# Eight weight copies instead of six behind the last token product: moving two weight loads of a fused recurrence and soft-MoE kernel

## The chip, the cores and the metric

The kernel runs on one core of one Trainium2 chip. The metric is the device time of one execution in microseconds (us). Four executions of the kernel before took 200.65, 200.97, 200.97 and 200.61 us, median 200.81 us. The core has five engines that run their own instruction streams: TensorE (PE in the profile; PEld is its weight load), VectorE (DVE), ScalarE (ACT), GpSimd (POOL) and SyncE (SP), which here only issues transfers. Transfers run on 16 DMA engines; in the profile q1 carries what SP issues, q0 what POOL issues.

## The reference

Two stages follow each other. The first is a gated recurrence over 5056 tokens for each of 4 sequences and 256 channels; the second is a soft mixture of experts over all 20224 tokens with 8 experts of 4 slots each.

```
f = lower_bound + (1 - lower_bound) * sigmoid(f_logit)
for t in range(S):  h = f[:, t] * h + (1 - f[:, t]) * x[:, t];  y[:, t] = h

logits = y @ phi                              # 20224 x 32
d = exp(logits);  d /= d.sum(over tokens)
slot_input = d.T @ y                          # 32 x 256
per expert e: slot_out = relu(slot_input[e] @ w1[e]) @ w2[e]
c = exp(logits);  c /= c.sum(over slots)
out = c @ slot_out
```

No output row can be written before the last token has gone through the recurrence, into `slot_input`, and through all experts. The expert weights `w1` (8 x 256 x 1024) and `w2` (8 x 1024 x 256) are 1 MB each per expert in float32, and are needed only then.

## The kernel before

**Units.** Tokens go in groups of 512 (`G`) per sequence; one group of one sequence is a *unit*, numbered n = 4 * group + sequence, so there are 40 units (0 to 39). A loop over n runs the stages of several units at once, shifted against each other. In the steady state iteration n issues, in this order: the loads of units n+6 and n+7 (`load`, lines 177 to 193, even n only, on SP); the sigmoid of units n+4 and n+5 on ACT (`gate`, line 203); the product of the sigmoid and x for unit n+3 on POOL (`enter`, line 214); weight copies, if any, on POOL (`load_w`, lines 128 to 134); then on PE the transposes of h of unit n-1 back to tokens (`to_tokens`, line 275), of the sigmoids of n+2 and n+3 and the product of n+1 to channels (lines 223 to 229); the decay factors on ACT (line 252); the recurrence itself as two scans of unit n on DVE (`scan`, line 262), 1.24 us each; the copy of unit n-1's tokens out of PSUM (line 292, DVE or ACT); and by groups the logits, exponentials and slot sums (lines 306, 315, 327 to 330, 356). Each engine executes its stream in the order in which the program writes it.

**Token buffers.** f and x arrive in tiles of two units; each of the two tags has three tiles (`ld`, line 149). The last x load, of units 38 and 39, is issued at n = 32 and takes the tile that the products of units 32 and 33 release; that release comes at n = 30.

**Weights.** There are 16 weight matrices, `w1[0..7]` and then `w2[0..7]`. `load_w(i)` issues a copy with a cast from float32 to bfloat16, from POOL, into a tile of its own; the last matrix is copied in two halves, so there are 17 copies. How many are issued at which iteration stands in the table `W_AT` (line 143), and a counter takes them in order:

```
            unit(enter, n + 3)
            for _ in range(W_AT.get(n, 0)):
                load_w(w_next[0])
                w_next[0] += 1
```

So the copies of iteration n stand behind the product of unit n+3 in POOL's stream. In the table of before, iterations 17 and 25 take `w1[0]` and `w1[1]`, 30 to 34 take `w1[2]` to `w2[1]`, and 36, behind the product of unit 39 (the last one), takes `w2[2]` to `w2[7]`. At most eight POOL transfers can be in flight: the program uses eight semaphores in turn for them, and a copy waits for the landing of the one eight before it.

**After the units.** Behind those copies POOL clears two tiles (`hid` and `wide`, lines 517 and 518) and copies the last 64 tokens' weights (`left`, line 349). PE finishes the last group's logits and slot sums, bridges waits with small matmuls whose result nobody uses (`spin`, line 139), then multiplies by the experts: line 566 with all of `w1`, line 602 with `w2[0..3]`, line 612 with `w2[4..7]` in four blocks of eight matmuls (j = 0 to 3, one matrix each; the last block waits for the halves of `w2[7]` separately). Between blocks j = 1 and j = 2 PE computes the row sums (line 339) and 14 spin matmuls. Line 627 (DVE) makes `slot_out`, on which all of the output depends. The output stage (lines 643 to 738) then multiplies `slot_out` into all tokens and writes 20.7 MB.

Of the kernel before, what the change touches and what calls it, by code (L numbers as in the profile page):

```python
# [18 lines left out]
def kernel(  # L19
# [108 lines left out]
    def load_w(i):  # L128
        if i < E:
            nc.gpsimd.dma_start(out=w1_sb[i], in_=w1_r[i])  # L130
        else:
            k = FC // 2 if i == 2 * E - 1 else FC
            for f in range(0, FC, k):
                nc.gpsimd.dma_start(out=w2_sb[i - E][:, ds(f, k)], in_=w2_r[i - E][:, ds(f, k)])
# [5 lines left out]
                             start=True, stop=True, skip_group_check=True)  # L140

    SPINS = 14
    W_AT = {17: 1, 25: 1, 30: 1, 31: 1, 32: 1, 33: 2, 34: 3, 36: 6}
    w_next = [0]
    ctx.enter_context(tc.manual_schedule())

# [3 lines left out]
    with tc.tile_pool(name="sp2", bufs=3) as sp2, \  # L150
# [211 lines left out]
        def unit(f, m):  # L362
            if 0 <= m < n_unit:
                f(m)
# [63 lines left out]
        for n in range(n_unit):  # L428
# [14 lines left out]
            else:  # L443
# [16 lines left out]
# [3 lines that stand above are left out]
# [306 lines left out]
```

## Time and profile before

| | |
|---|---|
| median of 4 executions | 200.81 us (200.61 to 200.97) |
| the profiled execution | 200.65 us, of it 198.9 us span |
| PE, DVE, ACT, POOL busy | 143.3, 142.4, 137.8, 102.5 us |
| read, written in HBM | 58.23 MB, 20.71 MB |
| q1 (token loads, outputs) | 62.13 MB, 76.6% of 16 engines' span |
| q0 (weights) | 8.42 MB counted at the destination, 21.1% |
| mean granted TensorE clock | 0.854 |

All positions below are microseconds from the start of the span. A line of a timeline reads: start, length, engine, line of the code, instruction, count, and in brackets how long the engine sat idle before it and what released it. A line of a table by stretches reads: stretch, its length, busy time and count of PE, PEld, DVE, ACT and POOL, the granted PE clock, the busy share of the DMA engines (values a little over 1.00 are to be read as full), and GB/s counted at the destination. For the casting weight copies the destination is half the source. A line of waits reads: who waited, for whom, total us, times, longest.

### The profile page before, as it was taken

Reading aid. Unit: us, or ns where it says so; the run is one execution under the profiler, and the core shown is the slowest. Engines: PE = TensorE matmul, PEld = TensorE weight load, DVE = VectorE, ACT = ScalarE, POOL = GpSimd, SP = SyncE. Lnnn points to the kernel's source line nnn. Section 1 sums busy time; section 2 is a strip of 40 time slices with the busy share of each in tenths; the row PEclk is TensorE's granted clock in tenths of the full one; section 3 lists DMA queues with packets and bytes.
Section 4 is the critical chain, followed back from the end, with each engine's and each line's share of the span. In section 5 each row is a group of like instructions: output and inputs, shape, how many; then the busy total and the mean of one; then the engine's idle time right before and its main releaser. Section 6 shows DMA issues by size and latency. Waiting matters only on the chain.

```text
span 198.9 us, 3264 instructions
## 1 busy us (share of the span) xinstructions
PE 143.3 (72%) x1201; PEld 103.6 (52%) x1201; DVE 142.4 (72%) x164; ACT 137.8 (69%) x194; POOL 102.5 (52%) x77
## 2 busy tenths in 40 slices
PE   0587594987978889778978565989989999950000
PEld 0365473965766769566866454666953643310000
DVE  2669878699999999999999978415168878840000
ACT  3688665999999999899985791434059889980000
POOL 2489596874999399947998547860030000000000
PEclk9999969699999999999999999799996555555555
DMA  5999999999999999999999999999629999999995
GB/s 187 415 419 420 422 417 419 420 419 417 416 420 419 335 392 419 416 361 356 413 369 273 283 247 216 214 213 212 127 96 425 421 436 422 428 458 428 422 422 214
DMA packets 17759, 70.76 MB, mean 356 GB/s; under 512 B 2112, under 2 KB 3136, under 8 KB 16848
## 3 DMA queue, kind: packets, MB, share of 16 engines
q1 hardware_dynamic: 15120, 62.13, 76.6%
q0 software_dynamic: 2480, 8.42, 21.1%
q8 instruction: 9, 0.15, 0.3%
q14 instruction: 6, 0.05, 0.1%
q10 hardware_dynamic: 144, 0.00, 0.0%
HBM read 58.23 MB, written 20.71 MB: 397 GB/s over the span
## 4 chain that ended last, share of the span: by engine, by line
PE 27%; DMA 25%; DVE 23%; issue 5%; ACT 3%; POOL 3%; SPq 1%; ACTq 0%; DVEq 0%; POOLq 0%
DVE h L262 19%; DMA x_t<-in_x_dram 15%; PE op L696 11%; DMA f_t<-in_f_logit_dram 11%; DVE ht L292 3%; POOL u_t L214 3%; PE op L647 2%; PE hp L275 2%; PE so_ps L612 2%; PE tail L139 1%; ACT oc L707 1%; ACT ob L641 1%; SPq L193 1%; PE up L229 1%; PE tail L339 1%
## 5 line engine op out<-in xcount | busy, mean ns | idle before, releaser
L214 POOL TENSOR_TENSOR u_t<-s_t,x_t 128x1024 bf16<-128x1024 bf16 (+1 forms) x39 | 82.4, 2129 | 26.0 <-ACT s_t L203 12.5
L262 DVE TENSOR_TENSOR_SCAN h<-a,h,up 128x512 bf16<-128x512 f32 (+1 forms) x72 | 85.8, 1244 | 3.8 <-PE up L229 2.3
L203 ACT ACTIVATE s_t<-f_t 128x2048 bf16<-128x2048 f32 (+2 forms) x23 | 38.6, 1677 | 10.4 <-DMA f_t<-in_f_logit_dram 10.4
L252 ACT ACTIVATE a<-sp,nomlb 128x1024 f32<-128x1024 bf16 (+2 forms) x46 | 43.3, 993 | 3.4 <-PE sp L229 3.0
L275 PE MATMUL hp<-ident_f,h 128*128 128x128 f32 (+1 forms) x160 | 30.6, 317 | 16.3 <-DVE ht L292 12.6
L275 PEld LDWEIGHTS hp<-ident_f,h 128*128 128x128 f32 (+1 forms) x160 | 23.3, 209 | 25.8 <-DVE ht L292 16.6
L229 PE MATMUL sp<-ident_f,s_t 128*128 128x128 f32 x144 | 21.0, 288 | 12.0 <-ACT s_t L203 9.0
L229 PE MATMUL up<-ident_f,u_t 128*128 128x128 f32 x144 | 24.0, 292 | 2.6 <-POOL u_t L214 2.5
L696 PE MATMUL op<-slot_bd,etall 64*128 64x512 bf16 x62 | 24.0, 586 | 0.6 <-ACT oc L707 0.3
L229 PEld LDWEIGHTS sp<-ident_f,s_t 128*128 128x128 f32 x144 | 16.9, 148 | 14.0 <-issue 5.8
L707 ACT ACTIVATE oc<-op,rrow 128x256 f32<-128x256 f32 x60 | 22.7, 488 | 1.5 <-PE op L696 0.9
L701 DVE TENSOR_TENSOR oc<-op,rrow 128x1024 f32<-128x1024 f32 x16 | 19.2, 1220 | 4.7 <-PE op L696 4.6
L229 PEld LDWEIGHTS up<-ident_f,u_t 128*128 128x128 f32 x144 | 18.2, 151 | 4.1 <-POOL u_t L214 3.6
L292 DVE COPY ht<-hp 128x512 f32<-128x512 f32 (+1 forms) x22 | 14.6, 666 | 4.1 <-PE hp L275 3.9
L696 PEld LDWEIGHTS <-etall 64*128 64x128 bf16 x62 | 9.0, 153 | 14.2 <-issue 11.7
L168 PE MATMUL slot_ps<-rep,ident 128*128 128x256 bf16 x112 | 16.2, 279 | 0.0
L292 ACT COPY ht<-hp 128x512 f32<-128x512 f32 (+1 forms) x18 | 10.6, 586 | 6.9 <-PE hp L275 6.8
L168 PEld LDWEIGHTS <-ident 128*128 128x128 bf16 x118 | 11.7, 103 | 1.9 <-issue 0.6
L641 ACT ACTIVATE ob<-op,rrow 128x256 f32<-128x256 f32 x16 | 6.3, 479 | 8.9 <-PE op L647 8.8
L262 DVE TENSOR_TENSOR_SCAN h<-a,up 128x512 bf16<-128x512 f32 x8 | 9.4, 1210 | 2.7 <-ACT a L252 2.0
L629 POOL TENSOR_SCALAR slot_bd<-slot_out,parity 128x256 bf16<-128x256 bf16 x2 | 1.8, 920 | 13.2 <-DVE slot_out L627 13.2
L306 PE MATMUL lg<-h,phi 128*32 128x512 bf16 (+1 forms) x80 | 7.7, 433 | 0.0
(99 smaller groups left out, 128.4 us busy)
## 6 DMA issues: line engine op xcount, KB each, us to landing
f_t<-in_f_logit_dram SPq DMA_DIRECT2D x36, 512.0 KB, 9.9
x_t<-in_x_dram SPq DMA_DIRECT2D x36, 512.0 KB, 9.9
out_dram<-oc SPq DMA_DIRECT2D x6, 2048.0 KB, 13.2
w_sb<-in_moe_w_dram POOLq DMA_DIRECT2D x15, 512.0 KB, 12.2
out_dram<-oc SPq DMA_DIRECT2D x4, 896.0 KB, 5.9
out_dram<-ob SPq DMA_DIRECT2D x1, 2048.0 KB, 8.9
f_t<-in_f_logit_dram SPq DMA_DIRECT2D x4, 384.0 KB, 9.1
x_t<-in_x_dram SPq DMA_DIRECT2D x4, 384.0 KB, 7.9
```

The costliest lines, as they stand in the source:

```text
L168: nc.tensor.matmul(slot_bank[:, 1, ds(0, rhs.shape[1])], ident, rhs, start=first and i < 2, stop=False, skip_group_check=True)
L203: nc.scalar.activation(s_t, f_t, ACT.Sigmoid, scale=-1.0)
L214: nc.gpsimd.tensor_tensor(uts[n][:, :r], s_t[:, :r], x_t[:, :r], ALU.mult)
L229: nc.tensor.transpose(ps[:, :, r], t[:, r], ident_f)
L252: nc.scalar.activation(decays[n // 2, o][:, ds(n % 2, k), :T], sp[:, ds(n % 2, k), :T, o], ACT.Identity, scale=nomlb[:, ds(o, 1)], bias=1.0)
L262: nc.vector.tensor_tensor_scan(h[:, :T, o], decays[n // 2, o][:, n % 2, :T], up[:, :T, o], hs[n - B][:, ds(used(n // B - 1) - 1, 1), o] if ...
L275: nc.tensor.transpose(hp[:n_p, r], hw[:, :n_p, r], ident_f)
L292: copy(hts[g][:n_p, b].rearrange("p r d -> p (r d)").bitcast(F32), hps.pop(n)[:n_p].rearrange("p r c -> p (r c)"))
L641: nc.scalar.activation(ob[:, i], op[:, i], ACT.Copy, scale=scale[:, i])
L696: nc.tensor.matmul(op[:, i_r].rearrange("p u d -> p (u d)"), ew[:, :, r + i_r], slot_bd[ds(j * 2 * NS, 2 * NS)].rearrange("s u d -> s (u d)"),
L701: nc.vector.tensor_tensor(ob[:, :, ds(r, k)].rearrange("p u r d -> p r u d"), op[:, ds(0, k)], scale[:, ds(r, k)].unsqueeze(3).broadcast_t ...
L707: nc.scalar.activation(ob[:, u, r + i_r], op[:, i_r, u], ACT.Copy, scale=scale[:, r + i_r, ds(u, 1)])
```

## The change

The table loses its entries for iterations 30 and 31, and the entry for 36 grows from 6 to 8.

```diff
-    W_AT = {17: 1, 25: 1, 30: 1, 31: 1, 32: 1, 33: 2, 34: 3, 36: 6}
+    W_AT = {17: 1, 25: 1, 32: 1, 33: 2, 34: 3, 36: 8}
```

Since the counter takes the matrices in order, the copies themselves keep their order, and the last `w2[7]` stays last. What changes is the place of each in POOL's stream: iterations 32 to 34 now take `w1[2]` to `w1[7]` (before: `w1[4]` to `w2[1]`), and all eight `w2` matrices, nine copies, stand behind the product of unit 39. The products of units 34 to 37 have two copies fewer before them. The instruction streams of PE, DVE, ACT and SP are the same, instruction for instruction.

## The prediction

> **What bounds the kernel now.** I read the chain of work that ended last first, in order of time (start, length, what).
>
> ```profile
> 99.21 21.05 DMA x_t<-in_x_dram
> 120.27 0.02 issue
> ...
> 120.42 2.16 POOL u_t L214
> ...
> 143.17 1.76 PE so_ps L612 x16
> 144.93 0.03 issue
> 144.96 0.06 DVE slot_out L627
> ```
>
> The last x load is on the chain for 21.05 us, against a median of 9.9 us for such loads; POOL's last product, PE's tail and `slot_out` at 144.96 follow. From there to the end everything hangs on `slot_out`. So the question is how much earlier `slot_out` comes. POOL's timeline shows what the load shared the DMA engines with:
>
> ```profile
> 98.75 0.57 POOL L130 DMA_DIRECT2D w_sb<-in_moe_w_dram  x1
> ...
> 101.44 0.58 POOL L130 DMA_DIRECT2D w_sb<-in_moe_w_dram  x1
> ...
> 110.84 1.07 POOL L134 DMA_DIRECT2D w_sb<-in_moe_w_dram  x2
> 116.69 2.14 POOL L214 TENSOR_TENSOR u_t<-s_t,x_t 128x1024 bf16<-128x1024 bf16 x1 [4.78 <-DMA x_t<-in_x_dram]
> 120.42 2.15 POOL L214 TENSOR_TENSOR u_t<-s_t,x_t 128x1024 bf16<-128x1024 bf16 x1 [1.59 <-DMA x_t<-in_x_dram]
> 122.51 3.23 POOL L134 DMA_DIRECT2D w_sb<-in_moe_w_dram  x6
> 126.41 0.53 POOL L134 DMA_DIRECT2D w_sb<-in_moe_w_dram  x1 [0.67 <-DMA w_sb<-in_moe_w_dram]
> ```
>
> Eight copies go out between 98.75 and 111.9. The products of units 38 and 39 wait 4.78 and 1.59 us for x. The last copy waits 0.67 us for an earlier one. The third view is the DMA by stretches:
>
> ```profile
> 100.00:120.00 20.00, 14.16 (x118) 11.51 (x115) 18.00 (x18) 15.24 (x16) 13.31 (x12) 1.00 1.06 288
> ...
> 126.00:128.00 2.00, 2.00 (x19) 1.30 (x18) 0.69 (x1) 0.73 (x2) 1.59 (x3) 0.74 1.08 217
> ...
> 142.00:144.00 2.00, 2.00 (x32) 1.90 (x31) 0.76 (x2) 0.00 (x0) 0.00 (x0) 1.00 0.27 49
> 144.00:146.00 2.00, 1.79 (x15) 1.28 (x13) 0.48 (x1) 0.00 (x0) 0.39 (x1) 1.00 0.03 8
> ```
>
> The reader is to see the second bound: the DMA engines are full from before 100 until about 142.5, and go idle only when the last weight is in. When that lands is read from SP, whose first output waits for the weights' memory:
>
> ```profile
> SPq L673 <- DMA w_sb<-in_moe_w_dram: 43.6, 2, 41.2
> ```
>
> SP issued its last load until 99.64 (98.84 plus 0.80). 41.2 us later, at 140.85, one matrix is in; the second wait adds 2.4, so the last half lands at 143.25. By the semaphores' order these are `w2[6]` and `w2[7]`. PE needs that last half for the last four of the 16 matmuls that end at 144.93, at 110 ns each, so from 144.49. The slack between weight stream and compute chain is 144.49 - 143.25 = 1.24 us. Two bounds lie that close together, and the change helps only one.
>
> **The change part by part.**
>
> *DMA work, conserved.* Nothing is removed. A weight (524 KB at the destination) takes 524/213 = 2.46 us alone (213 GB/s in the stretches from 120 on, DMA full), a load 524/420 = 1.25 us (about 420 GB/s in the load-only slices). After 120 the stretches move 4.73 MB, 9.0 weights; 14 went out from 98.75 on, so 5.0 passed between 100 and 120 (2.61 MB), and 5.75 - 2.61 = 3.14 MB were loads. Alone these would take 12.26 + 7.48 = 19.74 of the 20 us: mixing costs at most 0.26. Serving loads first therefore moves the end of the stream by 0 to 0.26 us earlier, if the engines never run dry. I take 0: landing stays at 143.25.
>
> *Does the stream run dry?* Without the copies at 98.75 and 101.44, the 3.14 MB of loads last until at least 107.5, and the copy of iteration 32 goes out near 102.8. The next five go out by 111.9 as before, since the product of unit 36 already waits 0.71 us for PE at 104.94 and absorbs what POOL gains. Six weights are 14.8 us of work; with the loads they fill the engines until 100 + 7.5 + 14.8 = 122.3. The nine `w2` copies can start when the product of unit 39 ends, about 116.3 (below). Margin 6 us.
>
> *Token loads.* Before x of unit 39 there are two weights fewer, 4.9 us: it lands at 115.4 instead of 120.27, and nearer 114 if the sharing stays as between 104 and 112 (272 to 289 GB/s, so weights about 70% of the time). The product of unit 38 can follow the copies at 112.0, that of 39 at 114.1 to 115.4, ending at 116.3 to 117.5 instead of 122.57.
>
> *What is late next.* DVE, by its timeline:
>
> ```profile
> 116.36 2.45 DVE L262 TENSOR_TENSOR_SCAN h<-a,h,up 128x512 bf16<-128x512 f32 x2 [1.30 <-PE up L229]
> 118.73 0.66 DVE L292 COPY ht<-hp 128x512 f32<-128x512 f32 x1
> 120.03 0.69 DVE L330 COPY et<-ep 128x1024 bf16<-128x1024 bf16 x1 [0.63 <-PE ep L327]
> 120.64 2.44 DVE L262 TENSOR_TENSOR_SCAN h<-a,h,up 128x512 bf16<-128x512 f32 x2
> ```
>
> Its 1.30 us wait goes back, through PE's transposes, to the sigmoid of units 38 and 39:
>
> ```profile
> ACT s_t L203 <- DMA f_t<-in_f_logit_dram: 1.2, 1, 1.2
> ```
>
> f of unit 39 is ahead of both x loads, so this wait goes; the exponentials and the token copy behind the sigmoid on ACT come 1.2 us earlier too. The 0.63 before line 330 goes with POOL's lateness, since PE's transposes of line 327 stood behind the late product of unit 38. With the 0.24 us before the scan of unit 39, DVE's last scan ends 1.3 to 2.1 us earlier (I take 1.9). PE's last long wait, 1.23 us for the product of unit 39 at 122.63, is replaced by DVE's line 330, ending 119.0; PE resumes its tail at 119.65 instead of 122.63, 2.98 us earlier. From there to `hi_ps` PE was busy nearly throughout, so 1.3 to 3.0 of it reach the experts. I take 2.9, as the scan then ends well before the logits of unit 39 need it.
>
> *Weights at the experts.* Counting back 2.46 us per matrix from 140.85, `w2[5]` lands at 138.4, `w2[4]` at 135.9, `w2[3]` at 133.5. Line 602 moves from 137.69 to 134.8 and finds its four; block j = 0 ends near 136.8; j = 1 waits for 138.4 and ends at 139.3; row sums (1.3) and spin (0.8) end at 141.4; j = 2 has `w2[6]` and ends at 142.3; the first half of j = 3 ends at 142.75, and the second waits for 143.25. It ends at 143.25 + 0.06 + 0.44 = 143.75 instead of 144.93. **Of 2.9 us, 1.18 remain.** Were the compute gain only 1.3, the result would be the same.
>
> *POOL.* Two issues of 0.57 leave the stretch to 102; two of 0.54 join behind unit 39. There the memsets, `left` and `slot_bd` queue behind them. The last copy waits, before and after, for the landing of `w2[0]` near 126 (eighth before it), which covers the 1.08 us, and the memsets still end near 131.4. If that cover is gone they end at 132.5; `wide` is first written at 137.84 - 2.9 = 134.9. The cost is 0 either way. SP's and ACT's queues are not passed.
>
> *Two rules against rows.* The weights run at 213 GB/s. The Trainium skill, "DMA: Bandwidth & Descriptors", section "Anatomy of one DMA — SWDGE (gpsimd) path", gives about 2 us plus bytes over 436 GB/s, an estimate of 1.2 us of engine time per copy; by it the stream would end long before line 612 and the whole 2.9 us would show, 197.7 us. The measured rate decides. The other rule is in the clock rival.
>
> **Sum.** Output stage and all after it shift by 1.18: 200.65 - 1.18 = 199.47 us for an execution like the profiled one. That execution lay 0.16 under the median of 200.81; the same shift from the median gives 199.63. I say 199.6.
>
> **The rivals.**
>
> *1. The clock (slower).* PE now waits about 1.6 us for `w2[5]`. The row: PE was busy 2.73 of the 6.1 us from 116.5 to 122.6, its longest gap 1.23 us, and the clock fell to 0.50 at about 123.6 for 3.6 us. If it falls at 138.4, j = 1, row sums, spin and j = 2, 3 (4.8 us) take up to 9.6: PE ends near 147.9, 3.0 later, 203.6 us. It decides if the clock falls before about 141; falling later, the gain merely shrinks. Against: from 136 to 141 PE would still be busy about two thirds, and a stretch with 0.71 busy of 3.2 us (111.6 to 114.8) kept the clock at 1.00. The Trainium skill, "TensorE: Matmul & The Clock Gate", section "HAM oscillation — how this bites in real kernels", asks for no idle gap over about 3.4 us; the trace fell with shorter ones. By that rule 1.6 us cost nothing. Middle price +1.5: 202.1.
>
> *2. The stream ends later (no change).* If the product of unit 39 ended after 122.3, the engines would idle, and each microsecond delays `w2[7]` and the end by one. A landing 0.8 to 1.5 us later gives 200.3 to 201.1. For: all nine copies now hang on that product. Against: the 6 us margin.
>
> *3. It does little for the tokens.* The six copies of 32 to 34 still run beside the last loads and take most of the time; if x of unit 39 lands after 119, the chain gains under 1 us: 199.9 to 200.6. Against: f and x of four units were ahead of any weight.
>
> *4. More than the forecast.* If mixing and the uneven last 1.5 us of the stream shrink, the landing comes 0.3 to 0.7 earlier: 198.9 to 199.3.
>
> **How the numbers follow.** Forecast 0.62 (199.2 to 200.1); clock 0.10; later stream 0.14; little for the tokens 0.06; more 0.08. About 0.2% (0.4 us) is what a measurement can tell from no change. Faster takes the forecast, rival 4, half of rival 3 and a little of rival 2: 0.75. Same: the rest of 3 and most of 2: 0.13. Slower: the clock and the end of 2: 0.12. The range runs from 199.0 to 201.0: out stay the clock's and the lowest values.
>
> **What would show it.** POOL's waits for x at units 38 and 39 mostly gone; DVE's 1.30 us gone; PE's last `hi_ps` block 2 to 3 us earlier; in line 612 a new wait for a weight; SP's wait for the weights ending again near 143.2; `slot_out` near 143.8. Wrong if the weights land later than 144, or the clock is under 1.00 between 137 and 144.

## The result and the profile after

The changed kernel takes 200.2 us in the median of 53 executions, the kernel before 200.97 us in the median of 79. The medians are 0.77 us apart. The ratio of the two is 0.9971, 95% interval 0.9959 to 0.9983: 0.3% faster, or 0.34 to 0.82 us. An execution over 1.5% above the fastest of its kernel is left out of a ratio, here and below (five of the ten of `no4_before`, at most two elsewhere). The forecast was 199.6 us, a gain of 1.18 us. The direction and the mechanism came out as forecast; about half of the gain did not come.

The profiled execution took 200.05 us, its span is 198.3 us. Its chain of work that ended last (start, length, what) no longer has a token load near the end:

```profile
113.40 4.18 POOL u_t L214 x2
117.58 8.81 DMA w_sb<-in_moe_w_dram
126.39 0.28 issue
126.67 16.97 DMA w_sb<-in_moe_w_dram
143.68 0.61 PE so_ps L612 x4
```

Where the last x load stood for 21.05 us, the chain now has two weight copies, and the last four matmuls of line 612 start when the second lands. POOL's timeline (start, length, instruction, idle before) shows why:

```profile
113.38 4.26 POOL L214 TENSOR_TENSOR u_t<-s_t,x_t 128x1024 bf16<-128x1024 bf16 x2 [1.69 <-PE hp L275]
117.58 3.23 POOL L134 DMA_DIRECT2D w_sb<-in_moe_w_dram  x6
121.72 0.53 POOL L134 DMA_DIRECT2D w_sb<-in_moe_w_dram  x1 [0.91 <-DMA w_sb<-in_moe_w_dram]
...
126.67 0.53 POOL L134 DMA_DIRECT2D w_sb<-in_moe_w_dram  x1 [1.91 <-DMA w_sb<-in_moe_w_dram]
```

The products of units 38 and 39 run back to back from 113.38 with no wait for x (before: 4.78 and 1.59 us); what holds them now is a wait of 1.69 us for PE. The nine copies behind them go out from 117.58. The last three each wait for a landing, and the last one goes out at 126.67, 0.26 after its place in the trace of before. DVE has no gaps left up to the last scan:

```profile
112.40 4.92 DVE L262 TENSOR_TENSOR_SCAN h<-a,h,up 128x512 bf16<-128x512 f32 x4
117.23 0.67 DVE L292 COPY ht<-hp 128x512 f32<-128x512 f32 x1
117.86 0.69 DVE L330 COPY et<-ep 128x1024 bf16<-128x1024 bf16 x1
118.47 4.78 DVE L262 TENSOR_TENSOR_SCAN h<-a,h,up 128x512 bf16<-128x512 f32 x4
```

The 1.30, 0.63 and 0.24 us waits are gone, and the last scan ends at 123.25 instead of 125.77. On PE the waits for weights took their place:

```profile
136.35 1.03 PE L612 MATMUL so_ps<-w_sb,wide 128*128 128x256 bf16 x8 [2.13 <-DMA w_sb<-in_moe_w_dram]
...
138.68 1.03 PE L612 MATMUL so_ps<-w_sb,wide 128*128 128x256 bf16 x8 [0.86 <-DMA w_sb<-in_moe_w_dram]
...
141.68 1.47 PE L612 MATMUL so_ps<-w_sb,wide 128*128 128x256 bf16 x12
143.68 0.60 PE L612 MATMUL so_ps<-w_sb,wide 128*128 128x256 bf16 x4 [0.53 <-DMA w_sb<-in_moe_w_dram]
```

Before, line 612 had no such wait. The expert stage starts far earlier (`hi_ps` at 129.55 instead of 134.11, 4.56 us), and most of that is given back in these three waits, 3.52 us together; another 0.40 is lost around them. `slot_out` starts at 144.32 instead of 144.96: 0.64 us, which is also the difference of the two spans (198.9 and 198.3). The DMA engines are full as before and go idle at the same place (stretch, length, busy times, PE clock, DMA share, GB/s):

```profile
100.00:120.00 20.00, 15.12 (x139) 12.44 (x138) 19.89 (x21) 14.86 (x16) 16.72 (x17) 1.00 1.06 290
...
142.00:144.00 2.00, 1.47 (x14) 1.17 (x12) 0.64 (x2) 0.00 (x0) 0.00 (x0) 1.00 0.17 32
```

They moved 290 GB/s between 100 and 120 against 288, and 32 against 49 in the last stretch: the end of the stream has hardly moved.

### The profile page after: what moved, and what is told of

It reads as the page before. It is cut to its first block, busy times and chain, and to the rows that moved or that the text cites. A ratio compares the mean times of both kernels' runs of the same rounds, so it can differ in the third digit from the quotient of the medians.

```text
span 198.3 us, 3264 instructions
## 1 busy us (share of the span) xinstructions
PE 142.9 (72%) x1201; PEld 103.7 (52%) x1201; DVE 142.3 (72%) x164; ACT 137.7 (69%) x194; POOL 102.5 (52%) x77
## 4 chain that ended last, share of the span: by engine, by line
DMA 31%; DVE 23%; PE 18%; ACT 8%; issue 7%; POOL 2%; ACTq 0%; DVEq 0%; SPq 0%; POOLq 0%
DVE h L262 18%; DMA w_sb<-in_moe_w_dram 13%; PE op L696 12%; DMA f_t<-in_f_logit_dram 10%; DMA x_t<-in_x_dram 8%; ACT a L252 3%; DVE ht L292 3%; POOL u_t L214 2%; PE op L647 2%; ACT s_t L203 2%; PE hp L275 1%; DVE ob L637 1%; ACT ht L292 1%; PE sp L229 1%; ACT L203 1%
## 5 line engine op out<-in xcount | busy, mean ns | idle before, releaser
L275 PE MATMUL hp<-ident_f,h 128*128 128x128 f32 (+1 forms) x160 | 29.6, 309 | 16.5 <-DVE ht L292 12.0
L275 PEld LDWEIGHTS hp<-ident_f,h 128*128 128x128 f32 (+1 forms) x160 | 22.8, 208 | 25.8 <-DVE ht L292 15.8
L229 PE MATMUL sp<-ident_f,s_t 128*128 128x128 f32 x144 | 22.3, 300 | 9.8 <-ACT s_t L203 7.5
L229 PEld LDWEIGHTS sp<-ident_f,s_t 128*128 128x128 f32 x144 | 18.0, 154 | 11.7 <-issue 5.7
L292 DVE COPY ht<-hp 128x512 f32<-128x512 f32 (+1 forms) x22 | 14.7, 670 | 1.7 <-PE hp L275 1.7
L168 PE MATMUL slot_ps<-rep,ident 128*128 128x256 bf16 x112 | 15.7, 273 | 0.0
```

The source lines that it names most:

```text
L168: nc.tensor.matmul(slot_bank[:, 1, ds(0, rhs.shape[1])], ident, rhs, start=first and i < 2, stop=False, skip_group_check=True)
L229: nc.tensor.transpose(ps[:, :, r], t[:, r], ident_f)
L275: nc.tensor.transpose(hp[:n_p, r], hw[:, :n_p, r], ident_f)
L292: copy(hts[g][:n_p, b].rearrange("p r d -> p (r d)").bitcast(F32), hps.pop(n)[:n_p].rearrange("p r c -> p (r c)"))
```

## Experiments

**Is the changed kernel bounded by the last weight, and the kernel before by the tokens?** The copies of `w2[4..7]` are taken away from both kernels, and line 612 multiplies by `w2[3]` in their place: the four matrices are left out of the output, the number of matmuls stays.

```diff
-    W_AT = {... 36: 8}          # before: 36: 6
+    W_AT = {... 36: 4}          # before: 36: 2
...
-                                 w2_sb[Q + j][:, fc],
+                                 w2_sb[Q - 1][:, fc],
```

> The changed table without the copies of w2[4..7]; the matmuls of line 612 use w2[3] instead, so the instruction count on TensorE stays and the last four experts' part of the output is computed from the wrong matrix. Theory (the changed kernel waits for the last weight, its compute chain is 3 to 4 us ahead): line 612 no longer waits, slot_out comes near 140.2 instead of 144.32 (34 matmuls, row sums and spin straight behind line 602 at 134.2), about 4.1 us less: 196.1 us. Rival (the compute chain is what ends last in the changed kernel too): at most 0.3 us less than the changed kernel.

> The table of before without the copies of w2[4..7], line 612 on w2[3]. Theory (before, the tokens bound, the weights land 0.9 to 1.2 us before they are needed): slot_out stays at 144.9, time within 0.3 us of the kernel before, since all eight copies ahead of the last tokens are still there. Rival (the weight stream bounded the kernel before as well): 3 to 4 us less.

The changed kernel without them: 196.43 us, ratio to before 0.9782 (0.9726 to 0.9838), 4.4 us. PE's timeline shows line 612 directly behind line 602, and DVE's shows `slot_out`:

```profile
134.28 1.05 PE L612 MATMUL so_ps<-w_sb,wide 128*128 128x256 bf16 x8
...
138.60 1.91 PE L612 MATMUL so_ps<-w_sb,wide 128*128 128x256 bf16 x16
```

```profile
140.55 0.48 DVE L627 TENSOR_SCALAR slot_out<-so_ps,rcs 128x256 bf16<-128x256 f32 x1 [0.99 <-PE so_ps L612]
```

So the changed kernel's compute chain is 3.8 us ahead of its weights, as the theory had it (4.1). The kernel before without the four copies: a median of 200.55 us over ten executions between 197.85 and 202.52, 0.36 under the 200.91 of the kernel before beside it; ratio 0.9927 (0.9877 to 0.9976). That is far from the 3 to 4 us of the rival, but past the "within 0.3" of the theory, a little by the medians and clearly by the ratio. In its profile `slot_out` starts at 143.60, 1.36 before the 144.96 that I had taken for the kernel before, with x still late (4.29 us wait). Of this, 0.26 us is an earlier start: PE begins the transposes of unit 39 (line 229) at 122.37 instead of 122.63. The other 1.10 lie between there and `hi_ps`, 10.39 us instead of 11.49. The rows by stretches show why; the first is of the kernel before, the others of this run:

```profile
123.50:127.20 3.70, 3.70 (x39) 2.15 (x40) 2.28 (x2) 1.80 (x4) 3.03 (x7) 0.54 1.06 213
```

```profile
114.00:116.00 2.00, 1.46 (x7) 1.46 (x8) 1.32 (x2) 1.97 (x3) 0.00 (x0) 0.62 1.09 272
116.00:118.00 2.00, 2.00 (x12) 1.75 (x11) 0.60 (x1) 2.00 (x4) 1.54 (x1) 0.53 1.08 246
123.50:127.20 3.70, 3.70 (x53) 2.46 (x53) 2.93 (x3) 2.42 (x6) 3.70 (x2) 1.00 1.06 214
```

The granted clock fell around 114.5 to 118 here, where TensorE waits for x anyway, and stayed at 1.00 from 123.5 to 127.2, where it was 0.54 in the trace of before: 53 matmuls passed there instead of 39. The stretch from line 229 of unit 39 to `hi_ps` takes 10.39 to 10.42 us in all eleven profiles of this document without a fall in it, 11.49 in that of before and 11.94 in that of `one_back` (below), which have one. So the end of the compute chain of the kernel before moves by more than a microsecond between executions. Where it ends early, that kernel too would meet the weights, and the change has less to win.

**How far does one have to go, and what is too far?** Only the table is changed, in both directions.

```diff
-    W_AT = {17: 1, 25: 1, 32: 1, 33: 2, 34: 3, 36: 8}
+    W_AT = {17: 1, 25: 1, 29: 1, 30: 1, 31: 1, 32: 1, 33: 2, 34: 3, 36: 5}   # one_ahead
+    W_AT = {17: 1, 25: 1, 31: 1, 32: 1, 33: 2, 34: 3, 36: 7}                 # one_back
+    W_AT = {17: 1, 25: 1, 32: 1, 33: 2, 36: 11}                              # three_more
```

> The opposite direction: one more copy ahead of the last tokens (one at 29, five at 36). Theory (on this side of the optimum the tokens end last, and each copy ahead of them is worth its 2.46 us of transfer time): x of unit 39 lands near 122.7 instead of 120.3, slot_out at 146.5 to 147.4, 1.5 to 2.5 us slower than before. Rival (only the end of the weight stream matters, since total transfer work is fixed): no change from before.

> Only the entry at 30 is moved: 31 keeps one copy, 36 takes seven. Theory (gain capped by the landing of the last weight, which one moved copy already reaches): tokens about 2.2 us earlier than before, last weight lands at 143.5 to 143.7, slot_out near 144.3 as in the full change, time 0.5 to 0.7 us below before. Rival (each moved copy brings its share): half the gain, 0.3 us.

> The three copies of 34 go behind the last product too: 36 takes eleven. Theory (total transfer work is fixed, so the stream ends later only by the time the DMA engines run dry): loads and the three remaining copies are worth 14.9 us from 100, the eleven are issued from about 117.3, so the engines are dry for 3 to 4.5 us, the last weight lands at 147 to 148, time 2.5 to 4 us above before. Rival (the tokens still bound, moving more copies helps more): equal to the changed kernel or faster.

| copies behind unit 39's product | median us | ratio to before | `slot_out` in the profile |
|---|---|---|---|
| 5 (one_ahead) | 203.88 | 1.0132 (1.0067 to 1.0197) | 148.63 |
| 6 (before) | 200.97 | 1 | 144.96 |
| 7 (one_back) | 200.39 | 0.9974 (0.9944 to 1.0004) | 144.54 |
| 8 (the change) | 200.2 | 0.9971 (0.9959 to 0.9983) | 144.32 |
| 11 (three_more) | 206.07 | 1.0253 (1.0177 to 1.0329) | 151.15 |

The ratios are to executions of the kernel before in the same run, with medians of 200.67 (5 copies) and 200.91 us (7 and 11). With 7 copies the last four matmuls wait for the same landing, by PE's timeline:

```profile
143.90 0.60 PE L612 MATMUL so_ps<-w_sb,wide 128*128 128x256 bf16 x4 [0.53 <-DMA w_sb<-in_moe_w_dram]
```

So the first moved copy already reaches the floor and the second adds nothing that can be measured, as the theory said (the interval of this run alone, though, would also admit the rival's half gain, or none; the trace decides). With 5 copies POOL waits longer for x than before:

```profile
121.45 2.14 POOL L214 TENSOR_TENSOR u_t<-s_t,x_t 128x1024 bf16<-128x1024 bf16 x1 [7.63 <-DMA x_t<-in_x_dram]
```

The product of unit 39 follows at 125.17. x came 4.75 us later, nearly twice the 2.46 that I had priced for one copy, and the time went past the 1.5 to 2.5 expected. The DMA queues show that the price was the wrong one. Between 100 and 104 the loads moved 0.77 MB here against 1.27 MB before. Beside copies they moved 1.62 MB in the 12 us from 104 to 116 of the trace of before, 0.135 MB per us, and at that rate the missing 0.50 MB take an estimated 3.7 us to catch up, not the 1.2 that they need alone. The release of the x tile is 0.6 later too (the loads go out at 99.44). How much of the rest is chance stays open: in the profile of `fill_before` (below), the same program as before up to that point, the products of units 38 and 39 also start 1.65 us later than in the trace of before.

With 11 copies the stream runs dry:

```profile
114.00:116.00 2.00, 1.38 (x13) 1.06 (x11) 1.98 (x2) 1.99 (x4) 2.00 (x2) 1.00 0.47 92
116.00:118.00 2.00, 1.63 (x16) 1.48 (x16) 2.00 (x4) 2.00 (x3) 2.00 (x2) 1.00 0.00 0
118.00:120.00 2.00, 1.27 (x22) 1.06 (x23) 2.00 (x4) 0.28 (x1) 2.00 (x5) 1.00 0.47 41
```

The DMA engines stand idle for about 4.1 us (1.06 + 2.00 + 1.06 of these six), which is the forecast size of that term. The last half then lands at 148.8 (issued at 131.31, 17.5 us by the list of transfers), past the 147 to 148 expected and 5.3 later than before. `slot_out` is 6.19 later in this profile (206.79 us, the slowest of four executions). The clock adds to the landing: from 136.6 to 150.3 it was at 0.50, PE waited for one matrix after another, and the last 16 matmuls of line 612 took 2.94 instead of 1.91 us, to 151.11.

**What has slack?** 18 more idle matmuls (1.95 us at full clock) stand where the changed kernel waits, and at the same place in the kernel before.

```diff
         for j in range(Q):
+            if j < 2:
+                spin(tail[:, 1], (12, 6)[j], D)
             for fc in range(FC):
                 nc.tensor.matmul(so_ps, wide[:, fc, j]...
```

> The changed kernel with 18 more idle matmuls of 256 columns on TensorE (1.95 us at full clock): 12 ahead of block j = 0 and 6 ahead of j = 1 of line 612, where it waits for weights. Theory (TensorE has 3 to 4 us to spare before the last weight): slot_out stays at 144.3, the added work costs nothing; and if the upper group of executions (200.9 to 201.7, 12 of 53) comes from the clock falling while TensorE waits for weights, that group thins out and the median falls by up to 0.3 us. Rival (TensorE's chain bounds the changed kernel): 1.5 to 2 us slower.

> The same 18 idle matmuls in the kernel before. Theory (before, the compute chain ends last): the 1.95 us lie on the path, slot_out at 146.5 to 146.9 instead of 144.96, 1.5 to 2 us slower than before. Rival (the weights bound the kernel before too): no change.

In the changed kernel they cost nothing: 199.96 us, ratio 0.9949 (0.9924 to 0.9974), `slot_out` at 144.11. In the kernel before they cost 1.0% (ratio 1.01, 1.0062 to 1.0137), 2.0 us, with `slot_out` at 147.47. That is 2.51 after the 144.96 of before and past the 146.5 to 146.9 expected: beside the 1.95 of the added work, line 602 already starts 0.55 later, since x came 1.65 later and the clock did not fall between line 229 and `hi_ps`. The same work is free in one and fully paid in the other, which shows the two bounds more directly than any wait. Executions of `fill` lay between 199.66 and 200.89, while the changed kernel on the same chip had two of twelve above 201; that fits the clock as a cause, but twelve executions don't show it.

**Can the last wait be shortened?** The last matrix comes in pieces of 4, 3 and 1 blocks, so that less work hangs on the last landing; then both edits together.

```diff
-            k = FC // 2 if i == 2 * E - 1 else FC
-            for f in range(0, FC, k):
+            f = 0
+            for k in (FC // 2, FC // 2 - 1, 1) if i == 2 * E - 1 else (FC,):
                 nc.gpsimd.dma_start(out=w2_sb[i - E][:, ds(f, k)], ...)
+                f += k
```

> The changed kernel with w2[7] copied in three pieces (4, 3 and 1 of its eight blocks) instead of two halves. Theory (after the last landing only the matmuls that need it are left): one matmul follows the landing instead of four, 0.3 us less than the changed kernel, slot_out near 144.0. Rival (the third copy's own fixed cost, or its 1 KB runs, delays the landing by as much): equal or up to 0.3 us slower.

> The changed kernel with both edits: w2[7] in pieces of 4, 3 and 1 blocks, and 18 idle matmuls where line 612 waits. Theory: slot_out near 143.8 as with the pieces alone, 0.4 to 0.7 us below the changed kernel; the idle matmuls take away executions above 200.9. Rival (the pieces' gain was spread between executions): equal to the changed kernel.

> The changed kernel once more, as the reference for the next three on the same chip. Both theories: 0.2 to 0.4% faster than before. In its profile the last half of w2[7] lands at 143.4 to 143.9 and the last four matmuls of line 612 follow it at once.

> The changed kernel a third time, as the reference on the same chip: 0.2 to 0.4% faster than before; the last half of w2[7] lands between 143.4 and 143.9.

The pieces alone: 199.67 us beside 200.3 of the changed kernel on the same chip; ratios to before 0.9945 (0.9912 to 0.9977) and 0.9971 (0.9942 to 1.0001). Both edits: 199.65 us beside 200.4, ratios 0.9928 (0.9897 to 0.9958) and 0.9983 (0.9944 to 1.0023). All twelve executions of `fill_split` lie between 199.27 and 199.81; the changed kernel's beside it between 199.75 and 202.64. PE's timeline of `fill_split` (line numbers moved by three):

```profile
143.19 0.62 PE L615 MATMUL so_ps<-w_sb,wide 128*128 128x256 bf16 x4 [0.18 <-DMA w_sb<-in_moe_w_dram]
```

The four matmuls start when the piece of three blocks is in; the last piece lands at 143.48 (issued at 128.78, 14.7 us by the list of transfers), and only the fourth needs it. `slot_out` starts at 143.85, 0.47 before the changed kernel's 144.32. From the last landing to `slot_out` 0.37 us pass instead of 0.68, which is the 0.3 us expected for fewer matmuls behind it; the other 0.16 is an earlier last landing, within what the profiles differ by. This version beats both kernels: eleven of the changed kernel's twelve executions took longer than its slowest, and so did all 23 of the kernel before in that run.

In the third profile of the changed kernel the rival of the clock came true, by the stretches:

```profile
136.00:138.00 2.00, 1.53 (x8) 1.10 (x9) 0.00 (x0) 0.00 (x0) 0.00 (x0) 0.61 1.11 221
```

The clock fell at 136.4, at the end of the wait for `w2[4]`, until 139.9; the 16 matmuls of j = 2 and 3 then ran without a wait (PE's timeline), and `slot_out` still came at 144.45:

```profile
142.42 1.99 PE L612 MATMUL so_ps<-w_sb,wide 128*128 128x256 bf16 x16
```

One fall of 3.4 us is thus just paid by the lead. In the second profile it fell at 146 instead, at the start of the output stage, and the first long block of matmuls (line 647) took 2.69 us against 1.90; that execution took 200.83 us with `slot_out` at 144.39, 0.78 more than the first with 144.32.

## Why the prediction was right and wrong

*Transfer work is conserved, the landing stays.* Right. The last waits for a weight end at 143.68 and 143.76 in two profiles with 8 copies, at 143.90 with 7, and at 143.48 with the idle matmuls. The stream did not run dry (share 1.06 from 100 to 120), and `three_more` shows what it costs when it does.

*Token loads, DVE, ACT.* Right in kind: the waits for x, the sigmoid's wait and DVE's gaps all went. The sizes were larger. x of unit 39 was in at 112.8 (99.21 plus 13.6 by its tile's transfers; forecast 114 to 115.4): 7.4 us earlier for two copies fewer, more than the 4.9 us of the copies' own transfer time. The slow rate of loads beside copies, shown with 5 copies above, fits that. The product of unit 39 ended at 117.64, 0.14 outside the forecast of 116.3 to 117.5, because of the new wait for PE. The last scan came 2.5 earlier (forecast 1.3 to 2.1).

*Compute lead.* Undersized: 4.56 us instead of 2.9. PE took up unit 39 at 119.16 (forecast 119.65), 3.47 earlier, and needed 10.39 us from there to `hi_ps` instead of 11.49, since it worked through 123.5 to 127.2 at full clock, where it had 0.54 before. The prediction left that fall out of its sum. It may not be chance that it went: PE was busy 5.32 of the 6.1 us from 116.5 to 122.6, before 2.73 (see the last section). The larger lead was without effect, since the weights cap it.

*"Of 2.9 us, 1.18 remain."* This is the step that failed, by size: the slack between the last landing and the compute chain before was taken as 1.24 us, and it was 0.81; 0.64 of that came as gain. Two readings are behind that:

- The landing before was taken as 143.25, by adding SP's two waits (43.6) to 99.64. That sum leaves out what lies between the two waits. The list of transfers has the last copy (issued at 126.41) as a row of its own, in KB and us to landing, and gives 143.51, 0.26 later than taken:

```profile
w_sb<-in_moe_w_dram POOLq DMA_DIRECT2D x1, 256.0 KB, 17.1
```

- The last four matmuls before were said to be needed from 144.49, at 0.11 us each. But a matmul here takes 0.27 us and the next starts 0.11 after its start, so four take 0.60 (3 x 0.11 + 0.27), as the four that follow the landing in the changed kernel do. Counted back by 0.60 from the end of the row before, they started at 144.32:

```profile
143.01 1.91 PE L612 MATMUL so_ps<-w_sb,wide 128*128 128x256 bf16 x16
```

In the terms of the sum, line 612 was to end at 143.25 + 0.06 + 0.44 = 143.75 and ended at 144.29, 0.54 later:

- 0.26 is the landing before, misread as above.
- 0.13 is that in the changed kernel it landed at 143.64 (126.67 plus 16.97, in the chain above). The spread of the four last waits above, 0.42, is wider than that, so it is no effect that could be shown.
- 0.15 is that from the landing to the end of the four matmuls 0.65 us passed (0.04 and 0.61), not 0.06 + 0.44.

*The base.* A second fault lies beneath: the slack was read from one execution. The kernel before has its compute chain in the open, so a fall of the clock there shows, and its executions lie between 199.85 and 202.75 us; the lowest is only 0.33 above the lowest of the changed kernel (199.52). Without the fall, 1.10 us, its last four matmuls would by estimate have been ready at 143.22, ahead of the landing at 143.51: such an execution is bounded by the weights already, and the change has next to nothing to win in it. The gain of a median is made of such cases too, not of the gap of one trace. That the ratio (0.58 us) came out close to the two profiled executions (0.64 us apart) is in part luck.

*The clock rival.* It happens, as `after_third` shows, but its price of 1.5 to 3.0 us was too high there: the clock fell for 3.4 us, not until the end, and the lead paid for it (`slot_out` at 144.45 against 144.32). What the executions of 202.6 to 202.8 us met is not shown. In `three_more`, where PE waits again and again, it stayed down for 13.7 us. The Trainium skill, "TensorE: Matmul & The Clock Gate", section "HAM oscillation — how this bites in real kernels", asks for no idle gap over about 3.4 us; in `after_third` the clock fell with a longest gap of 2.12 us, and in the trace of before with 1.23, so a shorter gap is no safeguard.

*POOL.* Right: the last copy at 126.67 and the memsets' end at 131.6 are within 0.26 of where they were. With the experts 4.56 earlier, ACT's copy at line 590 is put down as waiting 0.52 us for line 349 on POOL; before, it waited the same 0.52 for PE, so this cost nothing.

## What to carry to other kernels

Where the transfer queues are full from end to end, as here, reordering transfers moves time between the consumers and hardly the end of the stream (the last waits stayed between 143.48 and 143.90): find the landing of the very last one, and count what must still run after it; that difference caps the gain, whatever a long wait elsewhere looks like. Read such a landing from a row that states it, not from a sum of waits, and take a handful of matmuls after a wait at their full latency. Look at several executions of the kernel before for how far the other chain moves. When the cap is reached, make the last transfer small, so that less hangs on it.

## What the runs showed that was not expected

The falls of the granted clock to 0.50 come at different places, and the places differ between the two sides of the change. All five profiles in which POOL still waits for x have a fall between 114 and 127: from 114.5, 115.3, 116.7 and 123.6 with up to six copies behind unit 39's product, from 126.7 with 7. In the eight profiles in which x is on time (the changed kernel three times, the idle matmuls, the pieces, both, the run without the four copies, and the one with 11) the clock is at 1.00 from 100 to 136. The next falls there come at 136.4 and 136.6, where PE waits for weights, or with the output stage, from 143.5 on. Ahead of the output stage a fall lasts 3.4 us, or three and four times that (10.2 in `one_ahead`, 13.7 in `three_more`). These thirteen profiles suggest that the moved copies took the early fall away with the waits for x; no run changes those waits alone.

In a kernel bounded by TensorE's chain the time spreads over 2 us between executions (199.85 to 202.1 for all but one of 79); two sources are seen in the profiles, a fall between line 229 and `hi_ps` (1.1 us) and the landing of x (1.65 us later in `fill_before`). With idle matmuls in the waits, smaller last pieces and the chain off the path, the twelve executions of `fill_split` lay within 0.54 us. Neither edit alone did that (idle matmuls 199.66 to 200.89, pieces 199.19 to 201.03), and which of them did how much is not settled by so few executions.
